# One range flag for the whole core: combined by VectorE, read in two steps, and one store where there were two

## The chip, the cores and the metric

The kernel runs on one core of a Trainium2 chip. A core has five engines with queues of their own: TensorE (PE, with its weight loads as PEld), VectorE (DVE), ScalarE (ACT), GpSimd (POOL) and SyncE (SP, which here mostly issues DMAs). They meet only in semaphores. The metric is the device time of one execution in microseconds. Three runs of the kernel before took 266.16, 267.45 and 267.98 us, so the median is 267.45 us.

## The reference

Two stages in one function. First, attention inside chunks of 64 positions: 8 batches, 8 heads, 576 positions, 64 numbers per head.

```
scores = scale * q_c @ k_c^T                 # 64 x 64 per chunk and head
scores = scores - max(scores)
attn   = exp(scores) / (sum(exp) + 1e-9)
x      = attn @ v_c                          # back to [4608 tokens, 512]
```

Then a feed-forward layer on the 4608 tokens, with `w_in` [512, 2048] and `w_out` [2048, 512]:

```
h   = x @ w_in
out = (0.5 * h * (1 + erf(h / sqrt(2)))) @ w_out
```

All inputs and the output are float32.

## The kernel before

**Tiles.** The work is cut into nine tiles of 512 tokens. Tiles 0 to 7 are the first 512 positions of one batch each. Tile 8, the last one, takes what is left: the last 64 positions of all eight batches. A block of 128 of its rows is therefore two batches of 64 rows, which lie 576 rows apart in the output.

**Work on a tile.** Scores, exponentials, sums of exponentials, the products with `v`, the division, then the two large matrix products. These run as seven products of half blocks in place of eight; sums and differences of blocks are made by VectorE. Tile 8 does only the second half of this at the end of the kernel: its seven products with `w_out` (`mm2_seven`, matmuls on L761) are the last work of TensorE.

**The end of tile 8.** The seven products come in a fixed order. For the last tile it is: first product kept (L721); second product added to it (`done`, L726) and stored (`store_block`, L874) as the first quarter of the output; the product of `summed(1)` and the product of `summed(2)`, both kept; the product of `summed(4)`, added on VectorE and stored as the second quarter; the product of `summed(3)`, added in two pieces of 128 rows and stored as the third quarter; and the last product, which is accumulated in the same two PSUM banks as the `summed(3)` product and leaves in two pieces of 128 rows through `last_piece` (copy by VectorE on L978, stores on L981). Since the last product adds to the banks that VectorE has just read, TensorE waits for VectorE's reads on L726 before it starts each of its two pieces. Each piece of 128 rows is stored as two stores of 64 rows: SP issues one, ScalarE the other. In L874 the transfers are rearranged so that the 64 rows come first (`"m p d -> p m d"`).

**The range test.** The kernel leaves out the subtraction of the maximum. That is allowed while the sums of exponentials stay in range, so the reciprocals of all sums are kept in three places (`homes`), and `range_test` reduces each of them to its smallest and largest value per partition (L885), compares these with 2^-40 and 2^40 (L886, L887) and reduces the answers to one value per partition (`good`, L888). It is hooked in front of slot 6 of the last tile, that is, in front of the `summed(2)` product. After the last piece, `range_count` adds the 128 values up with a matmul by ones (L894), VectorE turns the count into an integer (L895), and all five engines load it into a register (L1337) and branch on it (L1338): if the count is under 128, `general()` does the whole computation again in the safe way. With these inputs it doesn't.

**The end of the program.** Past the branch, on lines that the profile puts at L1363, SP waits in turn for every semaphore that is still in use, the DMAs' among them, and then all engines meet in a last barrier.

**Order.** The schedule is written by hand: what an engine is to do stands in its queue in the order in which the Python code emits it.

Of the kernel before, what the change touches and what calls it, by code (L numbers as in the profile page):

```python
# [11 lines left out]
def kernel(  # L12
# [9 lines left out]
    nc = tc.nc  # L22
    P = 128
    f32 = mybir.dt.float32
    bf16 = mybir.dt.bfloat16
    Act = mybir.ActivationFunctionType

    B, H, S, D = q.shape
    CH = 64
# [3 lines left out]
    G = H // 2  # L33
# [4 lines left out]
    MT = CT * CH  # L38
# [22 lines left out]
    QD = P // G  # L61
# [17 lines left out]
    NB = MT // 32  # L79
    late = rest[:].bitcast(f32)[:, 256 - 14 * NB:256]  # L80
    homes = [None, ident_f[:], late]
# [26 lines left out]
    work = ctx.enter_context(tc.tile_pool(name="work", bufs=3))  # L108
# [5 lines left out]
    ps_at = ctx.enter_context(tc.tile_pool(name="ps_at", bufs=3, space=bass.MemoryType.PSUM))  # L114
# [414 lines left out]
    HD = d_model // 2  # L529
    HM = MT // P // 2  # L530
# [168 lines left out]
    def mm2_seven(t, hooks):  # L699
# [47 lines left out]
        for s, (name, left, right, then) in enumerate(steps):  # L747
            fresh = name not in bank
            for m in range(HM):
                for u in hooks.get(HM * s + m, ()):  # L750
                    u()
                split = last_tile and name == "a"
                if fresh and m == 0 and split:
                    bank["a"] = [ps_tp.tile([P, 1, HD], f32, tag="tp", name="y_ps") for _ in range(HM)]
                elif fresh and m == 0:
                    pool, tag = TP if name == "a" else MM
                    pool, tag = MM if last_tile else (pool, tag)
                    bank[name] = pool.tile([P, HM, HD], f32, tag=tag, name="y_ps")
                to = bank["a"][m][:, 0] if split else bank[name][:, m]
                for f in range(HF):  # L760
                    nc.tensor.matmul(to, left(f, m), right[:, f],  # L761
                                     start=(fresh and (split or m == 0) and f == 0),
                                     stop=(f == HF - 1), skip_group_check=True)
                if last_tile and s == len(steps) - 1:
                    last_piece(t, m, to)
            if then and not (last_tile and s == len(steps) - 1):
                then()
# [106 lines left out]
            by.dma_start(rows.rearrange("m p d -> p m d"), y_sb[i * CH:(i + 1) * CH])  # L874

    LOW, HIGH = 2.0 ** -40, 2.0 ** 40
    verdict = []

    def range_test():

        assert used == [h.shape[-1] for h in homes]
        n = len(homes)
        for a, op in enumerate((mybir.AluOpType.min, mybir.AluOpType.max)):
            for i, home in enumerate(homes):
                nc.vector.tensor_reduce(ends[:, a, i:i + 1], home, axis=mybir.AxisListType.X, op=op)  # L885
        nc.vector.tensor_scalar(ok[:, 0:n], ends[:, 0], LOW, None, op0=mybir.AluOpType.is_gt)  # L886
        nc.vector.tensor_scalar(ok[:, n:2 * n], ends[:, 1], HIGH, None, op0=mybir.AluOpType.is_lt)  # L887
        nc.vector.tensor_reduce(good, ok, axis=mybir.AxisListType.X, op=mybir.AluOpType.min)  # L888
        verdict.append(good)

    def range_count():

        count = ps_at.tile([1, 1], f32, tag="at", name="count")
        nc.tensor.matmul(count[:], ones_1, verdict[0], start=True, stop=True)  # L894
        nc.vector.tensor_copy(total, count[:])  # L895

    def general():

        SUBS = mybir.AluOpType.subtract
        for c in range(4):  # L900
            n = d_ff // 4
            raw = stage_tile()[:].rearrange("p (ks n) -> p ks n", ks=KS)
            nc.gpsimd.dma_start(raw, w_in_v[:, :, c * n:(c + 1) * n])
            DV(w_in_sb[:, :, c * n:(c + 1) * n], raw)
        for c in range(4):
            n = FF // 4
            raw = stage_tile()[:].rearrange("p (f n) -> p f n", f=n)
            nc.gpsimd.dma_start(raw, w_out_v[:, c * n:(c + 1) * n, :])
            DV(w_out_sb[:, c * n:(c + 1) * n, :], raw)
        with tc.For_i(0, B, 1) as b:  # L910
            with tc.For_i(0, S, CH) as s0:
                one_chunk(b, s0, SUBS)
# [63 lines left out]
    def last_piece(t, m, y_ps):  # L976
        y_sb = ypool.tile([P, HD], f32, tag="y", name="y_sb")
        DV(y_sb[:], y_ps)  # L978
        for i in range(P // CH):
            m0 = ((HM + m) * (P // CH) + i) * S + MT  # L980
            (nc.sync if i == 0 else nc.scalar).dma_start(out[m0:m0 + CH, 0:HD], y_sb[i * CH:(i + 1) * CH])  # L981

    def mm2_slot(t, ms, qt):
        st = tiles[t]
# [44 lines left out]
    def phase(t, extra2, by_rows=False, first=0, extra1={}, seven=False):  # L1029
        nms = MT // P  # L1030
        order = [(ms, qt) for ms in range(nms) for qt in range(NQ)]
        if by_rows:
            order = [(None, f) for f in range(FF - FC)] + [(ms, NQ - 1) for ms in range(nms)]
        if t not in DENSE:
            mm1_seven(t, extra1)
        else:
            for f in range(first, FF):
                for u in extra1.get(f, ()):
                    u()
                mm1_slot(t, f)  # L1040
        if seven:
            mm2_seven(t, extra2)
            return
        for s, (ms, qt) in enumerate(order):
            for u in extra2.get(s, ()):
                u()
            if ms is None:
                mm2_rows(t, qt)
            else:
                mm2_slot(t, ms, qt)  # L1050
        for u in extra2.get("end", ()):
            u()
# [33 lines left out]
    act_scratch = consts.tile([P, 1], f32, name="act_scratch")  # L1086
    small = consts.tile([P, 28], f32, name="small")
    ends = small[:, 0:6].rearrange("p (a i) -> p a i", a=2)
    ok, good, ones_1 = (small[:, 6:11].bitcast(bf16)[:, a:b] for a, b in ((0, 6), (6, 7), (7, 8)))
    total = small[0:1, 11:12].bitcast(mybir.dt.int32)  # L1090
    nc.gpsimd.memset(ones_1, 1.0)
    homes[0] = consts.tile([P, 3 * NB + 16 + 2 * NB], f32, name="early")[:]

    def act_table(func):
# [2 lines left out]
    with tc.manual_schedule():  # L1097
# [104 lines left out]
        mm, at = (ps_mm, "mm"), (ps_at, "at")  # L1202
# [53 lines left out]
        for t in range(1, NT):  # L1256
            n = t + 1
# [75 lines left out]
            if t == NT - 1:  # L1333
                e2.setdefault(6, []).append(range_test)
            phase(t, e2, first=5 if t == 1 else 0, extra1=e1, seven=True)
        range_count()
        in_range = nc.values_load(total)  # L1337
        with tc.If(in_range < P, preferred_fallthrough_block=False):  # L1338
            general()
# [1 line left out]
_INS = ['q', 'k', 'v', 'moe_w_in', 'moe_w_out']  # L1341
# [26 lines left out]
```

## Time and profile before

| what | us |
|---|---|
| median of three runs | 267.45 |
| profiled execution, its own time | 267.09 |
| its span, first to last instruction | 265.5 |
| TensorE busy | 256.1 |
| VectorE busy | 223.1 |
| ScalarE busy | 190.5 |
| end of the last copy of a result (L978) | 261.7 |

The profiled execution's own time is 1.6 us longer than its span, because the span leaves out what lies around the program. The profile lists instructions with start and duration; a name with a small q (SPq, ACTq) is the engine's sequencer, which waits, branches, loads registers and issues DMAs, and does not count as busy. The chain that ended last follows only work of engines and DMAs that it can link, so what happens after the last result has to be read from the sequencers' own rows.

### The profile page before, as it was taken

To read this page: it belongs to the slowest core of one execution; us is meant where nothing else is said; L and a number is where in the kernel's file an instruction comes from. 1 tells how busy PE (TensorE), PEld (TensorE's weight loads), DVE (VectorE), ACT (ScalarE), POOL (GpSimd) and SP (SyncE) were. 2 spreads that over 40 slices of the span, in tenths; PEclk is the share of its full clock that TensorE was granted. 3 is DMA by queue.
4 is the path that set the end of the run, shared out by engine and by line. 5 is a ranking of instruction groups with operands and counts; after the bars stand their busy time and mean duration, and the time that the engine had idled before them with its cause. 6 is when DMAs were issued, how large, how long until landed. Compare 5 with 4: busy or idle time off the path is not lost.

```text
span 265.5 us, 7854 instructions
## 1 busy us (share of the span) xinstructions
PE 256.1 (96%) x3122; PEld 210.6 (79%) x3122; DVE 223.1 (84%) x394; ACT 190.5 (72%) x386; POOL 103.2 (39%) x225
## 2 busy tenths in 40 slices
PE   6789999999999999999999999999999999999993
PEld 2478875556888888887888888888888888888882
DVE  6874986898897599678999999999999999948772
ACT  3856758987767987898888588947894789227720
POOL 7767778702364291481372095009411300000000
PEclk9999999999999999999999999999999999999998
DMA  6999998999979979999999988998973410130014
GB/s 201 268 311 396 395 401 236 283 193 289 243 195 284 220 175 244 275 239 249 276 245 232 267 186 237 217 175 195 264 160 80 134 42 2 41 119 3 2 40 125
DMA packets 123416, 54.02 MB, mean 203 GB/s; under 512 B 97776, under 2 KB 120304, under 8 KB 123376
## 3 DMA queue, kind: packets, MB, share of 16 engines
q1 hardware_dynamic: 123072, 53.23, 77.4%
q8 instruction: 25, 0.41, 0.7%
q10 hardware_dynamic: 304, 0.26, 0.3%
q14 instruction: 15, 0.12, 0.1%
HBM read 36.70 MB, written 9.44 MB: 174 GB/s over the span
## 4 chain that ended last, share of the span: by engine, by line
PE 76%; DMA 10%; ACT 7%; SPq 4%; issue 1%; DVE 0%; POOL 0%
PE hs_ps L601 31%; PE y_ps L761 22%; PE y_ps L791 13%; DMA arrival<-in_moe_w_out_dram 8%; ACT h L609 3%; SPq L181 2%; PE h_ps L491 2%; DMA arrival<-in_moe_w_in_dram 2%; PE av_ps L349 2%; PE h_ps L481 2%; ACT pT L272 2%; SPq L142 1%; PE y_ps L1025 1%; PE y_ps L989 1%; PE s_ps L264 1%; ACT L1095 1%
## 5 line engine op out<-in xcount | busy, mean ns | idle before, releaser
L609 ACT ACTIVATE h<-hs_ps 128x512 bf16<-128x512 f32 x87 | 49.6, 609 | 6.5 <-PE hs_ps L601 5.7
L238 POOL CAST v_nat<-arrival 128x256 bf16<-128x256 f32 x56 | 24.9, 473 | 33.5 <-DMA arrival<-in_v_dram 23.1
L601 PEld LDWEIGHTS <-w_in_sb 128*128 128x128 bf16 x348 | 33.9, 98 | 4.7 <-issue 0.2
L194 POOL CAST q_nat<-arrival 128x256 bf16<-128x256 f32 x40 | 16.8, 467 | 50.2 <-DMA arrival<-in_k_dram 25.3
L601 PE MATMUL hs_ps<-x,w_in_sb 128*128 128x256 bf16 x232 | 31.8, 272 | 0.0
L761 PEld LDWEIGHTS <-h 128*128 128x128 bf16 x240 | 23.2, 98 | 2.8
L1095 ACT ACT_TABLE_LOAD x16 | 20.5, 1283 | 1.3 <-PEq L1352 1.0
L190 POOL CAST k_nat<-arrival 128x256 bf16<-128x256 f32 (+1 forms) x44 | 19.1, 476 | 5.3 <-DMA arrival<-in_k_dram 5.3
L721 ACT COPY kept<-y_ps 128x512 f32<-128x512 f32 (+1 forms) x17 | 9.0, 536 | 16.0 <-PE y_ps L761 15.9
L761 PE MATMUL y_ps<-w_out_sb,h 128*128 128x256 bf16 x160 | 18.6, 273 | 0.0
L761 PE MATMUL y_ps<-v_bd,k_bd 128*128 128x256 bf16 x160 | 18.5, 273 | 0.1
L761 PEld LDWEIGHTS <-k_bd 128*128 128x128 bf16 x160 | 15.6, 98 | 2.1 <-issue 0.2
L618 ACT COPY hs_ps<-hs_ps 128x512 f32<-128x512 f32 x29 | 16.2, 583 | 0.6 <-PE hs_ps L601 0.5
L601 PE MATMUL hs_ps<-k_bd,w_in_sb 128*128 128x256 bf16 x116 | 16.6, 272 | 0.0
L493 ACT ACTIVATE h<-h_ps 128x512 bf16<-128x512 f32 x21 | 12.5, 604 | 5.5 <-PE h_ps L465 4.1
L272 ACT ACTIVATE pT<-s_ps 128x512 bf16<-128x512 f32 x28 | 14.4, 599 | 1.8 <-PE s_ps L264 1.8
L791 PEld LDWEIGHTS <-h 128*128 128x128 bf16 x144 | 13.8, 98 | 1.7
L465 PE MATMUL h_ps<-x,w_in_sb 128*128 128x256 bf16 x128 | 14.5, 273 | 0.1
L601 PE MATMUL hs_ps<-k_bd,w_in_more 128*128 128x256 bf16 x96 | 14.2, 273 | 0.0
L601 PEld LDWEIGHTS <-w_in_more 128*128 128x128 bf16 x128 | 12.5, 98 | 2.0 <-issue 0.3
L726 DVE TENSOR_TENSOR kept<-y_ps,kept 128x512 f32<-128x512 f32 (+1 forms) x16 | 10.4, 651 | 4.3 <-PE y_ps L761 2.3
L465 PEld LDWEIGHTS <-w_in_sb 128*128 128x128 bf16 x128 | 12.3, 98 | 2.1 <-DVE w_in_sb L1070 0.7
(175 smaller groups left out, 638.9 us busy)
## 6 DMA issues: line engine op xcount, KB each, us to landing
arrival<-in_v_dram SPq DMA_DIRECT2D x58, 128.0 KB, 3.2
arrival<-in_k_dram SPq DMA_DIRECT2D x28, 256.0 KB, 5.6
arrival<-in_q_dram SPq DMA_DIRECT2D x7, 1024.0 KB, 6.9
out_dram<-kept SPq DMA_DIRECT2D x24, 256.0 KB, 3.2
arrival<-in_moe_w_out_dram SPq DMA_DIRECT2D x4, 1024.0 KB, 12.1
arrival<-in_moe_w_in_dram SPq DMA_DIRECT2D x6, 512.0 KB, 8.5
out_dram<-y_sb SPq DMA_DIRECT2D x8, 256.0 KB, 2.5
arrival<-in_v_dram SPq DMA_DIRECT2D x28, 64.0 KB, 2.7
```

Source lines behind the costliest of these rows:

```text
L190: copy(st[nm][:, q0:q0 + n, g], st[nm + "f"][:, 2 * q0:2 * (q0 + n), g].rearrange("p (q r) d -> p q r d", r=2))
L194: copy(st[nm][:, g, j:j + 2].rearrange("p j r d -> p r j d"), st[nm + "f"][:, 2 * g:2 * g + 2, j:j + 2])
L238: copy(st["v"][:, r::2, n], st["vf"][:, r::2, n])
L272: nc.scalar.activation(pT[:].rearrange("p u (c j) -> p u c j", j=J), tiles[t]["s_ps"][m // 2][m % 2][:].rearrange("p u (j c) -> p u c j", ...
L465: nc.tensor.matmul(to[:, cols], left, right[:, cols], start=(start and a == 0), stop=stop, skip_group_check=True)
L493: nc.scalar.activation(tiles[t]["h"][:, f, :], h_ps[:], Act.Gelu)
L601: nc.tensor.matmul(hs[:, f], left[:, ks, f * P:(f + 1) * P], right[:, ks], start=(fresh and f == 0 and ks == 0), stop=(ks == 1), skip_grou ...
L609: nc.scalar.activation(h[:, n:n + HM, HD * c:HD * (c + 1)], src, Act.Gelu)
L618: "s11": lambda: AC(place_of("b")[:], bank["a"][:]),
L761: nc.tensor.matmul(to, left(f, m), right[:, f], start=(fresh and (split or m == 0) and f == 0), stop=(f == HF - 1), skip_group_check=True)
L791: nc.tensor.matmul(bank[name][:, m], left(f, m), right[:, f], start=(fresh and m == 0 and f == 0), stop=(f == HF - 1), skip_group_check=True)
L1095: nc.scalar.activation(act_scratch[:], rest[:, 0:1], func)
```

## The change

`range_test` now goes on after `good`: VectorE spreads `good` over 32 columns, transposes it in blocks of 32 by 32, reduces, combines the four blocks' values with three one-element minimums, and compares the result with 0.5. What comes out is one integer, `bad`. SP and GpSimd load it into a register there and then, at that place of their queues. Behind the last piece, VectorE copies it to another place (`bad_late`), and TensorE, VectorE and ScalarE load that copy. The matmul and the cast of `range_count` are gone, and so is the memset of the ones on GpSimd. The branch takes the register in place of the comparison with 128.

In `last_piece`, the first of the two pieces is stored with one store, issued by SP, in place of two by SP and ScalarE. Its target is written as [2 batches, 64 rows, 256 columns], its source as [128 partitions, 256 columns]. The second piece is stored by two stores as before.

```diff
-    verdict = []
...
     def range_test():
...
-        nc.vector.tensor_reduce(good, ok, axis=mybir.AxisListType.X, op=mybir.AluOpType.min)
-        verdict.append(good)
-
-    def range_count():
-
-        count = ps_at.tile([1, 1], f32, tag="at", name="count")
-        nc.tensor.matmul(count[:], ones_1, verdict[0], start=True, stop=True)
-        nc.vector.tensor_copy(total, count[:])
+        nc.vector.tensor_reduce(good, ok, axis=mybir.AxisListType.X, op=MIN)
+        turned = work.tile([P, NB, 32], f32, tag="rc", name="turned", bufs=4)[:, 0]
+        nc.vector.transpose(turned, good.to_broadcast([P, 32]))
+        nc.vector.tensor_reduce(good, turned, axis=mybir.AxisListType.X, op=MIN)
+        for s in range(1, G):
+            nc.vector.tensor_tensor(good[0:1], good[0:1], good[QD * s:QD * s + 1], op=MIN)
+        nc.vector.tensor_scalar(bad, good[0:1], 0.5, None, op0=mybir.AluOpType.is_lt)
+        read_flag(bad, (mybir.EngineType.SP, mybir.EngineType.Pool))
+
+    flag = nc.alloc_registers("flag")
+
+    def read_flag(source, engines):
+        for reg in flag:
+            if reg.engine in engines:
+                nc.reg_load(reg, source)
...
     def last_piece(t, m, y_ps):
         y_sb = ypool.tile([P, HD], f32, tag="y", name="y_sb")
         DV(y_sb[:], y_ps)
-        for i in range(P // CH):
-            m0 = ((HM + m) * (P // CH) + i) * S + MT
-            (nc.sync if i == 0 else nc.scalar).dma_start(out[m0:m0 + CH, 0:HD], y_sb[i * CH:(i + 1) * CH])
+        n = P // CH
+        to = out.rearrange("(b s) d -> b s d", s=S)[(HM + m) * n:(HM + m + 1) * n, MT:S, 0:HD]
+        if m < HM - 1:
+            nc.sync.dma_start(to, y_sb[:])
+            return
+        for i, by in enumerate((nc.sync, nc.scalar)):
+            by.dma_start(to[i], y_sb[i * CH:(i + 1) * CH])
...
-    ok, good, ones_1 = (small[:, 6:11].bitcast(bf16)[:, a:b] for a, b in ((0, 6), (6, 7), (7, 8)))
-    total = small[0:1, 11:12].bitcast(mybir.dt.int32)
-    nc.gpsimd.memset(ones_1, 1.0)
+    ok, good = small[:, 6:12], small[:, 12:13]
+    bad = small[0:1, 13:14].bitcast(mybir.dt.int32)
+    bad_late = act_scratch[0:1, 0:1].bitcast(mybir.dt.int32)
...
-        range_count()
-        in_range = nc.values_load(total)
-        with tc.If(in_range < P, preferred_fallthrough_block=False):
+        nc.vector.tensor_copy(bad_late, bad)
+        read_flag(bad_late, (mybir.EngineType.PE, mybir.EngineType.DVE, mybir.EngineType.Activation))
+        with tc.If(flag, preferred_fallthrough_block=False):
             general()
```

More of the change, by code (lines that the diff above doesn't have):

```diff
@@ L876 @@
     LOW, HIGH = 2.0 ** -40, 2.0 ** 40
-    verdict = []
     def range_test():
         assert used == [h.shape[-1] for h in homes]
-        n = len(homes)
+        MIN, n = mybir.AluOpType.min, len(homes)
         for a, op in enumerate((mybir.AluOpType.min, mybir.AluOpType.max)):
```

## The prediction, made before the result was known

> **What bounds the kernel now.** I read the page first, then the chain that ended last from 225 us on, then the rows of the sequencers behind its end.
>
> ```profile
> span 265.5 us, 7854 instructions
> ...
> PE 76%; DMA 10%; ACT 7%; SPq 4%; issue 1%; DVE 0%; POOL 0%
> ```
> ```profile
> 248.99 12.24 PE y_ps L761 x112
> 261.23 0.02 issue
> 261.26 0.42 DVE y_sb L978
> 261.68 0.05 DVE small L895
> ```
>
> TensorE sets the time up to 261.2 us. The chain stops at 261.7, the span at 265.5: 3.8 us follow in which no compute engine works. The whole change lies in this tail and in the 7 us ahead of it, so I take the tail apart. The timeline gives the last stores' issues (start, length); the views of single lines give the rest (shortest/median/longest in ns, first and last start); the view of DMAs, cut to the last two issues, gives KB and the time from issue to landing.
>
> ```profile
> 260.83 1.36 SPq L981 DMA_DIRECT2D out_dram<-y_sb  x2
> 260.84 1.42 ACTq L981 DMA_DIRECT2D out_dram<-y_sb  x2
> ```
> ```profile
> L1337 POOLq TENSOR_LOAD <-small x1: 587/587/587, 261.8 to 261.8; - x1
> ...
> L1337 SPq TENSOR_LOAD <-small x1: 952/952/952, 262.2 to 262.2; - x1
> L1337 ACTq TENSOR_LOAD <-small x1: 920/920/920, 262.3 to 262.3; - x1
> ```
> ```profile
> L1338 SPq COMPARE_BRANCH  x2: 38/50/61, 263.3 to 263.4; - x2
> ```
> ```profile
> L1363 SPq EVENT_SEMAPHORE  x12: 28/28/28, 263.9 to 264.6; - x12
> ```
> ```profile
> L1363 SPq DRAIN  x3: 7/7/13, 264.7 to 265.0; - x3
> ```
> ```profile
> out_dram<-y_sb SPq DMA_DIRECT2D x1, 64.0 KB, 1.9
> out_dram<-y_sb ACTq DMA_DIRECT2D x1, 64.0 KB, 2.2
> ```
>
> SP issues its last store until 262.2, loads the flag for 0.95 us until 263.2, branches twice, and starts its list of twelve waits at 263.9, 0.5 us behind the branch. The twelve follow each other at (264.6 - 263.9) / 11, about 0.06 us, and end at 264.6; the last barrier takes 0.9 us more. The last stores were issued at 261.7 and landed at 263.6 (SP) and 263.9 (ScalarE). So **SP's own walk is last, and the stores land 0.7 us before its list ends**. That 0.7 us is all that shortening SP's walk can bring.
>
> **The change part by part.** *SP's load moves forward.* It frees 0.95 us behind the last store. SP would then begin its list at 262.9, and the landing at 263.9 becomes the last event. Which of the twelve waits is for that landing isn't shown; behind it follow none to seven others at 0.06 us (eight DMA semaphores stand among the last eight waits), so the list ends between 263.9 and 264.4. Gain, if the stores land as they do now: 0.2 to 0.7 us; middle 0.45.
>
> The trace backs the price of the load only for its old place. The Trainium skill, "DMA: Bandwidth & Descriptors", section on latency and other measured facts, gives such a load a floor of about 600 ns; GpSimd's 587 ns agrees and SP's 952 ns is longer. By the 600 alone SP's list would begin 0.35 us later than I reckon, at 263.25, and still reach its last waits about when the landing comes.
>
> *What the load meets at its new place.* SP waits there for VectorE's flag, and the stores of the second and third quarter stand behind it in SP's queue.
>
> ```profile
> 256.54 0.16 DVE L888 TENSOR_REDUCE small<-small 128x1 bf16<-128x6 bf16 x1
> 257.82 1.24 DVE L726 TENSOR_TENSOR kept<-y_ps,kept 128x512 f32<-128x512 f32 x2 [1.12 <-PE y_ps L761]
> 259.51 0.42 DVE L726 TENSOR_TENSOR kept<-y_ps,kept 128x256 f32<-128x256 f32 x1 [0.45 <-PE y_ps L761]
> ```
> ```profile
> L885 DVE TENSOR_REDUCE small<-early x2: 244/246/247, 254.9 to 255.6; 128x1 f32<-128x96 f32 x2
> ...
> L885 DVE TENSOR_REDUCE small<-rest x2: 373/374/374, 255.3 to 255.9; 128x1 f32<-128x224 f32 x2
> ```
> ```profile
> L287 DVE STREAM_TRANSPOSE pt<-pT x16: 431/434/437, 132.5 to 212.9; 128x256 f32<-128x256 f32 x16
> ```
> ```profile
> L309 DVE STREAM_TRANSPOSE rc<-rest x12: 690/700/712, 165.3 to 228.8; 128x512 f32<-128x512 f32 x12
> ```
> ```profile
> L299 DVE TENSOR_TENSOR total<-part x16: 214/216/220, 141.8 to 216.2; 32x64 f32<-32x64 f32 x16
> ```
> ```profile
> 261.60 0.13 DVE L895 CAST small<-count 1x1 int32<-1x1 f32 x1
> ```
>
> Six operations are added on VectorE. The transposes cost 434 ns at 256 columns and 700 at 512, so about 1.04 ns a column and 0.17 us to start: 0.20 at 32 columns. The reductions, 246 at 96 and 374 at 224, give 0.18 at 32. A one-element minimum lies between the one-element cast (0.13) and L299 (0.22): I take 0.15, three times. The comparison I put at L888's 0.16. Each waits for the one before, 0.03 us apiece: sum 0.20 + 0.18 + 0.45 + 0.16 + 0.18 = 1.2 us. `good` ends at 256.7, the flag at 257.9. VectorE is idle until 257.8 (the 1.12), so its next additions slip by 0.1 us, and the idle 0.45 before the third absorbs that.
>
> SP loads from 257.9 for 0.6 to 0.95 us. Its next store was issued at 258.5 and now goes at 258.65 to 258.9.
>
> ```profile
> 253.30 7.26 SPq L874 DMA_DIRECT2D out_dram<-kept  x5
> ```
> ```profile
> out_dram<-kept SPq DMA_DIRECT2D x3, 128.0 KB, 2.4
> ```
>
> The five issues end at 260.56, and an issue is 0.6 us long; three of them from 258.9 end at 260.8, just in time for the first piece at 260.84. GpSimd loads at the same time and has nothing behind it but its branch. Moving the load costs nothing.
>
> *The matmul and cast go; a copy comes.* L895 starts at 261.60, behind the last copy on VectorE; the new one-element copy stands in the same place. TensorE, VectorE and ScalarE load as before. ScalarE's load ends at 263.2, well before the end of SP's list. Zero, and zero for the memset, which ended at 1.3 us on a GpSimd that later waits for a DMA:
>
> ```profile
> 1.22 0.10 POOL L1091 MEMSET small<- 128x1 bf16 x1
> ...
> 4.71 0.61 POOL L196 CAST k_nat<-arrival 128x512 bf16<-128x512 f32 x1 [0.32 <-DMA arrival<-in_k_dram]
> ```
>
> *The joined store.* Its issue takes SP 0.6 us in place of 0.49, from 260.84 to 261.45; the last piece is due at 261.7. That is free. The shape isn't free, as I see it: its target counts 2 batches first, then 64 rows. All other stores of tile 8 put 64 rows first (L874 turns its blocks round for it), all loads of the code 16, 64 or 128 partitions. If a transfer is divided among the 16 DMA engines along the first count, this one can use two of them, 64 KB each. The price of that comes from these rows (the seventh field is the DMA engines' share, the last GB/s):
>
> ```profile
> 261.90:262.20 0.30, 0.00 (x0) 0.00 (x0) 0.00 (x0) 0.00 (x0) 0.00 (x0) 1.00 1.06 368
> ```
> ```profile
> 262.00:263.00 1.00, 0.00 (x0) 0.00 (x0) 0.00 (x0) 0.00 (x0) 0.00 (x0) 1.00 0.76 245
> ```
> ```profile
> q1 hardware_dynamic: 123072, 53.23, 77.4%
> ```
>
> One DMA engine moves 368 / 16 = 23 GB/s in the busiest moment, 245 / (16 x 0.76) = 20.1 in the last us, and 53.23 MB / (16 x 0.774 x 265.5 us) = 16.2 over the run. 64 KB take 2.85, 3.25 and 4.05 us by these; I take 3.25, from the stage itself. A usual store of 128 KB lands after 2.4 us, 0.4 of which is the 8 KB of each engine. So this one lands after 2.4 - 0.4 + 3.25 = 5.25 us, at 260.84 + 5.25 = **266.1**. SP's half of the last piece stands behind it on those two engines with 4 KB each, 0.2 us: 266.3. SP's list then ends 0 to 0.4 us later, at 266.5, and the span at 266.5 + 0.9 = 267.4 in place of 265.5. The gain in front is covered wholly. Sum: **+1.9 us**, with the other rates +1.5 and +2.7.
>
> No row decides whether the first count divides the transfer. The Trainium skill says so: in "DMA: Bandwidth & Descriptors", section on why a DMA increments its semaphore by 16, a copy runs on the largest number of engines up to 16 that divides the slowest counts of both sides, here 2 and 128, so two engines. The same page of the Trainium skill, in its rules for kernel authors, calls two transfers of partition halves no better than one of 128 partitions, which speaks for joining; by that the sum would be -0.45. No run here shows either.
>
> **The forecast.** Against the profiled execution, 267.09 + 1.9 = 269.0. That execution lies 0.36 below the median of the three runs, within their spread of 1.8; from the median, 267.45 + 1.9 = 269.35, and I say **269.3 us**.
>
> **The rivals.** *The joined store spreads over all engines (other side).* For it: its source has 128 partitions, and a 128 KB store with 128 target rows lands in 2.4 us. Then it lands at 263.2, ahead of the last piece at 263.9, and the end gains 0.45: 267.0 us. It decides at the landing: up to about 264 the store is hidden, past it each us counts in full.
>
> *The flag chain overruns VectorE's gap.*
>
> ```profile
> 257.56 1.91 PE L761 MATMUL y_ps<-v_bd,s_sb 128*128 128x256 bf16 x16
> 259.31 1.91 PE L761 MATMUL y_ps<-v_bd,h 128*128 128x256 bf16 x16
> ```
>
> TensorE's last product starts at 259.31 and needs the bank that VectorE's second addition has read by 257.82 + 1.24 = 259.06. That leaves 0.25 us. If each of the six cost as much as the narrowest transpose of the trace (0.43, with waits 2.8), the flag would come at 259.5, 1.7 late, and TensorE would stall 1.4. A milder half of it, 0.7, on top of the forecast gives 270.0. Against it: the rows scale well with width.
>
> *The early read changes nothing*, because the branch or the list waits for an engine that reads late, and the store is spread: 267.45.
>
> **How the numbers follow.** The forecast 0.68, the spread store 0.22, the overrun 0.07, nothing 0.03. I give the forecast three times the spread store's chance because the code takes care to put rows first everywhere else. Its own range is +1.0 to +2.9, that is 268.4 to 270.3: the two other rates and half a us of scatter. It holds less than 8 in 10 alone, so the range reaches down to the spread store: 266.5 to 270.3. A change of 1%, 2.7 us, is about what a measurement of this kernel tells from none. Only the slow rate or an overrun passes +2.7: slower 0.17; faster by 1% would need more than the tail can lose: 0.01; within 1%: 0.82.
>
> **What would show it.** Right: the joined store's landing above 4.5 us, low DMA share at a rate near 40 GB/s from 263 to 266, SP's list stopping at one wait near 266, no flag load behind SP's last issue. Spread: landing near 2.4, list ending near 264.2. Overrun: a gap on TensorE before its last sixteen matmuls, with L726 as what ended it. The prediction is wrong above all if two engines are more than two.

## The result and the profile after

With the change the kernel takes 268.32 us (median of 22 runs, 267.70 to 270.13), against 266.58 us for the kernel before (22 runs, 265.52 to 269.38). The ratio is **1.007, with a 95% interval of 1.005 to 1.0089**: 0.7% slower, about 1.8 us. The forecast was a loss of 1.9. The forecast time of 269.3 us lies 1.0 us above the measured one; 0.9 of that comes from its start, the median of three runs of the kernel before, 267.45, where 22 runs give 266.58.

The profiled execution of the changed kernel took 270.0 us by its own time, with a span of 268.4. That is 2.9 us more than the profiled execution before, and not all of it is the change. The end of the chain shows how to split it:

```profile
262.28 0.02 issue
262.30 0.42 DVE y_sb L984
262.73 0.05 DVE act_scratch L1346
```

The last copy of a result ends at 262.73, where it ended at 261.68 before. This 1.05 us is there before the range test begins: the last of the stores on L867 that leave from `y_sb` is issued at 237.4 before and at 238.5 after, while the first of them, at 98.5 before, goes out at 97.8 after. Executions of one and the same kernel differ by as much (the runs above). What follows the last copy, up to the end of the span, is steadier. I call it the **tail**: 265.54 - 261.68 = 3.86 us before, 268.36 - 262.73 = 5.63 after, +1.77 us. The tail alone accounts for the result (+1.74 us between the medians), and in it the experiments below are read to a tenth of a us, where the timed ratios have intervals of half a us and more to each side.

SP's issues of the last two pieces, from the timeline, and the landings of the last two stores, from the view of DMAs cut to their issues:

```profile
261.88 0.62 SPq L988 DMA_DIRECT2D out_dram<-y_sb  x1
262.76 0.52 SPq L991 DMA_DIRECT2D out_dram<-y_sb  x1
```
```profile
out_dram<-y_sb SPq DMA_DIRECT2D x1, 64.0 KB, 4.4
out_dram<-y_sb ACTq DMA_DIRECT2D x1, 64.0 KB, 4.6
```

The halves of the last piece landed after 1.9 and 2.2 us before; now they take 4.4 and 4.6. SP's list of twelve waits (cut at 263.9 to 267.45), and what held it up by the view of waits of SP:

```profile
L1373 SPq EVENT_SEMAPHORE  x12: 28/28/1039, 264.0 to 267.4; - x12
```
```profile
SPq L1373 <- DMA out_dram<-y_sb: 1.8, 2, 1.3
SPq L1373 <- ACTq L901: 1.1, 1, 1.1
```

The list ran through in 0.7 us before. Now it spans 3.4 us and is held by the last stores twice, 1.8 us in all. (The 1.1 us on ScalarE's load comes before that and costs nothing: the stores land later still.) Finally, here are the stages behind 262 us, with the DMA engines' share and GB/s as the last two columns:

```profile
262.00:263.00 1.00, 0.27 (x3) 0.00 (x0) 0.47 (x2) 0.00 (x0) 0.00 (x0) 1.00 0.81 196
263.00:264.00 1.00, 0.00 (x0) 0.00 (x0) 0.00 (x0) 0.00 (x0) 0.00 (x0) 1.00 0.39 133
264.00:265.00 1.00, 0.00 (x0) 0.00 (x0) 0.00 (x0) 0.00 (x0) 0.00 (x0) 1.00 0.22 43
265.00:266.00 1.00, 0.00 (x0) 0.00 (x0) 0.00 (x0) 0.00 (x0) 0.00 (x0) 1.00 0.68 188
```
```profile
263.60:264.50 0.90, 0.00 (x0) 0.00 (x0) 0.00 (x0) 0.00 (x0) 0.00 (x0) 1.00 0.12 42
```

From 263.6 to 264.5 the DMA engines are busy to 0.12, and 0.12 of 16 is two. Their rate of 42 GB/s is 21 GB/s for each, about the 20.1 of one engine from 262 to 263 in the kernel before. The other fourteen idle in that stretch, although the last piece's stores have been issued at 262.76.

The trace holds one more sign, which no view prints: the single events by which a landing is counted. The stores with 64 rows first have sixteen each. The joined store has three: one at 262.88 and two at 266.83, 4.95 us after its issue, and SP's list passes its wait only behind those two. The other two kernels with such a store show three as well.

### The profile page after: what moved, and what is told of

It is laid out like the page before. It is cut to its first block, busy times and chain, and to the rows that moved or that the text cites. A ratio compares the mean times of both kernels' runs of the same rounds, so it can differ in the third digit from the quotient of the medians.

```text
span 268.4 us, 7853 instructions
## 1 busy us (share of the span) xinstructions
PE 256.7 (96%) x3115; PEld 210.8 (79%) x3121; DVE 224.6 (84%) x400; ACT 190.5 (71%) x386; POOL 104.3 (39%) x224
## 4 chain that ended last, share of the span: by engine, by line
PE 80%; ACT 7%; DMA 6%; SPq 3%; DVE 1%; issue 1%
PE hs_ps L601 30%; PE y_ps L761 22%; PE y_ps L791 13%; DMA arrival<-in_moe_w_in_dram 4%; ACT h L609 3%; PE h_ps L465 3%; PE y_ps L1035 3%; PE h_ps L491 2%; SPq L181 2%; PE av_ps L349 2%; DMA arrival<-in_q_dram 2%; PE h_ps L481 2%; ACT pT L272 2%; PE y_ps L999 1%; PE s_ps L264 1%; PE y_ps L465 1%
## 5 line engine op out<-in xcount | busy, mean ns | idle before, releaser
L190 POOL CAST k_nat<-arrival 128x256 bf16<-128x256 f32 (+1 forms) x44 | 20.3, 503 | 5.2 <-PE hs_ps L601 3.5
L605 DVE TENSOR_TENSOR hs_ps<-hs_ps,kept_p 128x512 f32<-128x512 f32 x15 | 10.3, 691 | 3.4 <-PE hs_ps L601 3.1
```

What stands on the lines that cost most here:

```text
L190: copy(st[nm][:, q0:q0 + n, g], st[nm + "f"][:, 2 * q0:2 * (q0 + n), g].rearrange("p (q r) d -> p q r d", r=2))
```

## The experiments

Each kernel was timed 10 to 12 times next to 35 runs of the kernel before on the same chip. The diffs are against the changed kernel, except that of the joined store alone, which is against the kernel before.

**The flag's part alone.** The first piece goes out by two stores again.

```diff
-        n = P // CH
-        to = out.rearrange("(b s) d -> b s d", s=S)[(HM + m) * n:(HM + m + 1) * n, MT:S, 0:HD]
-        if m < HM - 1:
-            nc.sync.dma_start(to, y_sb[:])
-            return
-        for i, by in enumerate((nc.sync, nc.scalar)):
-            by.dma_start(to[i], y_sb[i * CH:(i + 1) * CH])
+        for i in range(P // CH):
+            m0 = ((HM + m) * (P // CH) + i) * S + MT
+            (nc.sync if i == 0 else nc.scalar).dma_start(out[m0:m0 + CH, 0:HD], y_sb[i * CH:(i + 1) * CH])
```

> The flag's part alone: the first of the last two pieces goes out by two stores again, one from SP and one from ScalarE. Theory A (the joined store runs on two DMA engines, and its landing is the end): no landing above 2.7 us, SP's list ends between 0.2 and 0.7 us earlier relative to the last copy than in the kernel before, so the ratio to the kernel before is 0.9975 to 0.9995, about -0.45 us. Theory B (the early flag on VectorE and SP is what costs): the loss of 1.7 us stays, ratio about 1.007.

Measured: 0.9999 (0.9973 to 1.0024), which decides against theory B but cannot tell the small gain from nothing. The tail can:

```profile
262.13 0.42 DVE y_sb L984
262.55 0.05 DVE act_scratch L1342
```
```profile
L1369 SPq EVENT_SEMAPHORE  x12: 27/28/28, 263.7 to 265.0; - x12
```
```profile
out_dram<-y_sb SPq DMA_DIRECT2D x1, 64.0 KB, 2.0
out_dram<-y_sb ACTq DMA_DIRECT2D x1, 64.0 KB, 2.3
```
```profile
SPq L1369 <- DMA out_dram<-y_sb: 0.6, 1, 0.6
```

The span ends at 265.95, so the tail is 3.40 us, 0.46 less than before. SP's list starts 1.2 us behind the last copy (263.7 - 262.55; it was 2.2 before), and the last line, from the view of SP's waits, shows that it is now held once, for 0.6 us, by the landing of a store. The trace's events say which: SP's own store of the last piece lands at 264.56, the list's fifth wait passes at 264.58, and the seven behind it end at 265.0. ScalarE's store, landed at 264.85, is the twelfth and holds nothing. The flag's part does what its working said: it takes SP's load off the end, and a landing takes its place.

**The same once more**, for the interval.

> The flag's part alone, a second time, for a tighter interval. The profile of the first time gave a tail of 3.4 us behind the last copy, 0.46 less than in the kernel before, while the timed ratio 0.9999 could not tell that from nothing. Theory A: tail 3.3 to 3.5 us again, ratio 0.9975 to 0.9995.

Measured: 0.9973 (0.9951 to 0.9996), tail 3.38 us. The tail is the same to 0.02 us; the two ratios lie on either side of what it says (0.47 of 266.6 us is 0.9982).

**The joined store alone**, in the kernel before:

```diff
-        for i in range(P // CH):
-            m0 = ((HM + m) * (P // CH) + i) * S + MT
-            (nc.sync if i == 0 else nc.scalar).dma_start(out[m0:m0 + CH, 0:HD], y_sb[i * CH:(i + 1) * CH])
+        n = P // CH
+        to = out.rearrange("(b s) d -> b s d", s=S)[(HM + m) * n:(HM + m + 1) * n, MT:S, 0:HD]
+        if m < HM - 1:
+            nc.sync.dma_start(to, y_sb[:])
+            return
+        for i, by in enumerate((nc.sync, nc.scalar)):
+            by.dma_start(to[i], y_sb[i * CH:(i + 1) * CH])
```

> The joined store alone, on the kernel before: the flag is counted by TensorE and loaded late by all engines, as before. Theory A: the joined store lands about 5 us after its issue, the whole loss is here, ratio 1.006 to 1.009; SP's late load of 0.95 us is hidden behind that landing, so the loss is not larger than that of the whole change. Theory B: ratio within 0.002 of 1.

Measured: 1.0063 (1.0040 to 1.0086), tail 5.88 us. The whole loss is here, and the joined store lands 5.06 us after its issue by its events. One part of the expectation did not hold in the tail: it is 0.25 us longer than that of the whole change, with the last two landings at 4.5 and 4.8 us in place of 4.4 and 4.6. The loads of the flag, which all five engines make behind the last result in this kernel, show something that neither theory speaks of:

```profile
L1341 PEldq TENSOR_LOAD <-small x1: 486/486/486, 263.9 to 263.9; - x1
L1341 ACTq TENSOR_LOAD <-small x1: 2131/2131/2131, 264.4 to 264.4; - x1
L1341 SPq TENSOR_LOAD <-small x1: 2157/2157/2157, 264.4 to 264.4; - x1
```

The two engines that have just issued a store wait over 2 us for one number, TensorE 0.49 us. SP's load still costs nothing here: its list starts at 267.2, and the landings hold it twice more.

**Two stores, both by SP**, so that ScalarE's half moves to SP and nothing is joined:

```diff
-            nc.sync.dma_start(to, y_sb[:])
+            for i in range(n):
+                nc.sync.dma_start(to[i], y_sb[i * CH:(i + 1) * CH])
             return
```

> The whole change, but the first piece goes out by two stores of 64 rows that SP issues both. Theory A: each lands in about 2.0 to 2.4 us, nothing above 3 us; SP's issues take 2 x 0.5 us in place of 0.62, so its last store goes out about 0.2 us later than that of ScalarE; the time is that of the flag's part alone plus 0 to 0.3 us, ratio 0.998 to 1.000. Theory C (it is SP's queue that is too long when ScalarE's half moves there): ratio stays near 1.007.

Measured: 1.0007 (0.9981 to 1.0033), tail 3.78 us, and no landing above 2.7 us. Theory C falls: SP's queue alone doesn't cost 1.8 us. The price of the fuller queue is 0.4 us against the flag's part alone, a little more than the 0 to 0.3 expected, because SP's half of the last piece goes out later than reckoned, at 260.75 where the last copy ended at 260.37:

```profile
259.52 1.14 SPq L989 DMA_DIRECT2D out_dram<-y_sb  x2
260.75 0.55 SPq L992 DMA_DIRECT2D out_dram<-y_sb  x1
```

**One store with the rows first.** The two halves of the piece are copied next to each other on 64 partitions, so that one store of 128 KB counts 64 rows first.

```diff
-        y_sb = ypool.tile([P, HD], f32, tag="y", name="y_sb")
-        DV(y_sb[:], y_ps)
...
         if m < HM - 1:
-            nc.sync.dma_start(to, y_sb[:])
+            turned = ypool.tile([P, HM, HD], f32, tag="y", name="y_turned")
+            for i, copy in enumerate((DV, AC)):
+                copy(turned[0:CH, i], y_ps[i * CH:(i + 1) * CH])
+            nc.sync.dma_start(to.rearrange("b s d -> s b d"), turned[0:CH])
             return
+        y_sb = ypool.tile([P, HD], f32, tag="y", name="y_sb")
+        DV(y_sb[:], y_ps)
```

> The whole change, still one store of 128 KB for the first piece, issued by SP, but with 64 rows as the first count: the two halves of the piece are copied next to each other on 64 partitions (one half by VectorE, one by ScalarE). Theory A: it lands in about 2.4 us as every store with 64 or 128 rows first, and the time is that of the flag's part alone, ratio 0.997 to 1.000. Theory D (one store of 128 KB in place of two is what lands late, whatever its shape): landing near 5 us, ratio near 1.007.

Measured: 0.9961 (0.9939 to 0.9983), tail 3.32 us; the ratio is a little below the range expected. One store of the same 128 KB, by the same queue, costs nothing when 64 rows are counted first. Theory D falls. The DMA engines' share stays high until the data run out in the third of these stages:

```profile
261.00:262.00 1.00, 0.00 (x0) 0.00 (x0) 0.18 (x2) 0.00 (x0) 0.00 (x0) 1.00 0.71 205
262.00:263.00 1.00, 0.00 (x0) 0.00 (x0) 0.00 (x0) 0.00 (x0) 0.00 (x0) 1.00 0.91 250
263.00:264.00 1.00, 0.00 (x0) 0.00 (x0) 0.00 (x0) 0.00 (x0) 0.00 (x0) 1.00 0.18 38
```

Two small shifts cancel in this tail. SP's last store goes out 0.26 us behind the last copy, where it was 0.03 in the flag's part alone. Its landing is now the list's twelfth wait, though, so the seven waits that followed it there, 0.4 us, do not come on top.

**The same once more**, because 0.4% is more than the tail explains.

> One store of 128 KB with 64 rows first, a second time, since it came out 0.4% faster than the kernel before while its tail, 3.3 us, is only 0.5 us (0.2%) shorter. If the tail is all there is to it: ratio 0.997 to 0.999. If it has another gain that the tail doesn't show: ratio near 0.996 again.

Measured: 0.9974 (0.9952 to 0.9996), tail 3.33 us, and the joined store lands as SP's other stores of 128 KB do:

```profile
out_dram<-y_turned SPq DMA_DIRECT2D x1, 128.0 KB, 2.4
```

Both intervals lie below 1, so this kernel beats the kernel before and the changed one. How far is known only from the tail, 0.53 us or 0.2%; whether there is a gain beyond it, these runs leave open.

**Half the bytes on the two engines.** The joined store takes half the columns; the rest goes out by two stores of 64 rows.

```diff
-            nc.sync.dma_start(to, y_sb[:])
+            half = HD // 2
+            nc.sync.dma_start(to[:, :, 0:half], y_sb[:, 0:half])
+            for i, by in enumerate((nc.sync, nc.scalar)):
+                by.dma_start(to[i, :, half:HD], y_sb[i * CH:(i + 1) * CH, half:HD])
             return
```

> The whole change, but the joined store carries only half the columns of the first piece (64 KB in rows of 512 B); the other half goes out by two stores of 64 rows. Theory A (two engines, and the time is that of their data): 64 rows of 512 B on each of two engines take about 0.6 of the time of rows of 1 KB, so the joined store lands in 3.4 to 4.0 us in place of 4.95, and the tail behind the last copy is 4.2 to 5.0 us (3.86 in the kernel before, 5.63 with the change). Theory E (the cost is per row handed out, not per byte): landing stays near 4.9 us, tail near 5.6.

Measured: 1.0030 (1.0001 to 1.0058). The last copy ended at 262.28, the span at 266.9: the tail is 4.62 us, in the middle of theory A's range. Above the flag's part alone (3.39, the mean of its two tails) that is 1.23 us, where the whole joined store costs 2.24. Half the bytes give 0.55 of the price, with as many rows. The landing events put the joined half at 3.4 us from its issue, at the lower edge of what was expected. In the trace's DMA records a packet of 512 B takes 27 ns and one of 1 KB 46 ns, which is the 0.6 of the expectation. Theory E falls.

**A longer flag chain.** Two stores for the first piece, and eight more minimums on VectorE.

```diff
+        for _ in range(8):
+            nc.vector.tensor_tensor(good[0:1], good[0:1], good[QD:QD + 1], op=MIN)
         nc.vector.tensor_scalar(bad, good[0:1], 0.5, None, op0=mybir.AluOpType.is_lt)
...
         if m < HM - 1:
-            nc.sync.dma_start(to, y_sb[:])
+            for i, by in enumerate((nc.sync, nc.scalar)):
+                by.dma_start(to[i], y_sb[i * CH:(i + 1) * CH])
             return
```

> The flag's part alone (two stores for the first piece), with eight more one-element minimums in the flag's chain on VectorE, 0.18 us each, 1.45 us in all. By the working of the prediction VectorE's gap is used up to 0.05 us by the chain as it is and TensorE has some 0.25 us of slack behind it, so TensorE stalls about 1.1 us ahead of its last sixteen matmuls and the end moves by as much: about +0.7 us against the kernel before, and 0.4 to 1.2 are within the theory. If the chain is free as long as SP and GpSimd alone wait for it: no stall, -0.4 us.

Measured: 1.0044 (1.0024 to 1.0063), about +1.2 us, the upper edge of what was expected. The timeline of TensorE:

```profile
259.47 1.91 PE L761 MATMUL y_ps<-v_bd,s_sb 128*128 128x256 bf16 x16
262.29 1.91 PE L761 MATMUL y_ps<-v_bd,h 128*128 128x256 bf16 x16 [0.91 <-DVE kept L726]
```

Sixteen matmuls follow each other at 1.75 us elsewhere in this stage (257.56 and 259.31 before); here 2.82 us lie between the two starts, so TensorE stalls 1.07 us, on the additions of L726, as worked out. The stall less the shorter tail (3.71 in place of 3.86) makes 0.92 us, inside the measured interval (0.6 to 1.7 us). The tail did not shorten by the 0.4 us expected: SP's last store lands 2.3 us after its issue here, 2.0 in the flag's part alone.

## Why the prediction was right, point by point

**What bounds the end.** Right. The kernel's time before was set by SP's walk: the flag's part alone shortens the tail by 0.46 and 0.48 us, where the middle of the sum was 0.45, and the landing of SP's last store takes over. Which of the twelve waits is for it, the prediction could not tell: it is the fifth.

**The joined store on two engines.** Right, and now shown: the share of 0.12 from 263.6 to 264.5, the two landing events at 266.83, the loss with the joined store alone, no loss with two stores by the same queue or with one store that counts rows first. The rule of the Trainium skill, "DMA: Bandwidth & Descriptors", section on why a DMA increments its semaphore by 16, by which the slowest counts of both sides set the number of engines, agrees with the trace: two of sixteen engines. The same page of the Trainium skill, in its rules for kernel authors, advises one transfer of 128 partitions in place of two of halves; measured here, that one transfer alone cost 1.7 us (ratio 1.0063) with 2 batches counted first, and the one store that cost nothing lay on 64 partitions.

**Its price.** The sum was right to 0.13 us; its terms were off by more, in ways that cancel, and that they cancel is luck. Counted from the end of the last copy, the last landing was put at 266.3 - 261.68 = 4.62 us; 262.76 + 4.6 - 262.73 gives 4.6. But the joined store itself landed earlier than put, and the last piece's halves later behind it. SP's list passes the waits that were left at 266.8 and 267.4:

```profile
L1373 SPq EVENT_SEMAPHORE  x2: 28/28/28, 266.8 to 267.4; - x2
```

The first of these follows the joined store's landing, 4.95 us from its issue in place of 5.25. The halves were to follow 0.2 us behind and followed 0.5 us behind. The sum put only SP's half on the two busy engines, 4 KB on each; ScalarE's half has as much there, which by the same rate makes 0.4. Of the list there was one wait left behind the last landing, 0.06 us in place of the 0.2 taken. The tail came to +1.77 against +1.9.

**The flag's chain on VectorE.** Right to the size: 1.2 us worked out, and 258.93 - 257.74 = 1.19 measured.

```profile
257.58 0.16 DVE L887 TENSOR_REDUCE small<-small 128x1 f32<-128x6 f32 x1
257.78 0.21 DVE L889 STREAM_TRANSPOSE turned<-small 128x32 f32<-128x32 f32 x1
258.02 0.19 DVE L890 TENSOR_REDUCE small<-turned 128x1 f32<-128x32 f32 x1
258.24 0.51 DVE L892 TENSOR_TENSOR small<-small 1x1 f32<-1x1 f32 x3
258.79 0.14 DVE L893 TENSOR_SCALAR small<-small 1x1 int32<-1x1 f32 x1
258.90 1.21 DVE L726 TENSOR_TENSOR kept<-y_ps,kept 128x512 f32<-128x512 f32 x2
```

Widths of 256 and 512 columns foretold the transpose at 32 (0.20 against 0.21), and 96 and 224 the reduction (0.18 against 0.19). TensorE did not stall (its last two groups of sixteen start 1.75 us apart, 258.61 and 260.36); the rival of an overrun did not happen, and the longer chain shows that its edge lay within 0.1 us of where it was put: 1.45 us more brought 1.07 of stall, 1.15 by the working.

**SP's load at its new place.** Right that it costs nothing; it took 0.48 us there, less than either end of the range given:

```profile
L901 SPq TENSOR_LOAD <-small x1: 477/477/477, 259.0 to 259.0; - x1
```

**The chances.** A change within 1% was called likely, and 0.7% is that. But with 22 runs a side the measurement tells 0.2% from nothing on this kernel, so 1% was too coarse a bound for what could be told.

## What to carry to other kernels

Before two transfers are joined, look at the count that comes first in the joined shape, not at the bytes: here 2 batches ahead of 64 rows put 128 KB on two of sixteen DMA engines and turned a gain of 0.46 us into a loss of 1.8, and the same bytes in one store with the rows first kept the gain. Only the counts 2 and 64 were run. Where the last stores end a kernel, measure the tail behind the last result by itself: in the two kernels that were profiled twice it repeated to 0.02 us, where whole runs of a kernel scatter by 2 to 4 us. And a small chain on an engine is free only up to the point where another engine waits for what stands behind it; here that point was some 0.4 us away (1.45 us added, 1.07 us of stall).

## What the runs showed of the hardware that I had not expected

In the changed kernel the joined store holds up the stores issued after it, on the idle engines and on the other queue too. SP and ScalarE issue the last piece from 262.76 on, fourteen engines are idle, and yet only two work until 264.5. The busy microsecond is 265 to 266. By the landing events, fourteen of the sixteen parts of SP's half had landed by 266.12, 3.36 us after its issue; before, all sixteen had after 1.95. So they were held for about 1.4 us, but not until the joined store was through at 266.83. As far as these events tell, the hold did not set the end: the last to land, from 267.00 to 267.34, are the two remaining parts of each half, behind the joined store's data. The hold came again with the joined store alone, where every part of SP's half landed 3.1 us or more after its issue. With half the bytes on the two engines it did not: fourteen parts of ScalarE's half of the last piece had landed after 2.2 us, as all sixteen had before. What holds the stores was not settled.

A load of a register behind the issue of a held store takes longer as well: 2.05 us on ScalarE here,

```profile
L901 ACTq TENSOR_LOAD <-act_scratch x1: 2050/2050/2050, 263.4 to 263.4; - x1
```

where it took 0.89 us behind a store of 64 rows in the flag's part alone. It ended at 265.4, about when the DMA engines became busy again. Over all runs without a hold, a load right behind a store of 64 rows took 0.66 to 0.95 us, and one on an engine that had not just issued a store 0.47 to 0.80 us. So a part of SP's 0.95 us in the kernel before may be the price of its place behind a store: three engines that had issued none loaded the same number there in 0.59 to 0.61. How much of it is, these overlapping ranges leave open.
